# Rearranged start, output projection and shared weight buffers in a fused attention and MLP kernel

## The chip, the cores and the metric

The kernel runs on one core of a Trainium2 chip. The metric is the device time of one execution in microseconds (us). The core has a matrix engine (TensorE, PE in the profile, with its weight loads shown as PEld), a vector engine (VectorE, DVE), an activation engine (ScalarE, ACT), GpSimd (POOL) and a sync engine (SyncE, SP). In this kernel SP's queue issues every DMA.

## The reference

The input x has 2048 rows of 1024 values in bfloat16. The reference applies a layernorm, a dilated local attention with 32 heads of 32 values, and a residual addition, and then a second layernorm, a bilinear gated MLP with 3584 hidden values, and a second residual addition. Each position attends to eight positions: itself and those 2, 4, ... 14 rows earlier.

```python
h  = x + attention(layernorm(x), wqkv, wo)
h2 = h + mlp(layernorm(h), w_gate, w_up, w_down)

# attention: W, dil = 8, 2
idx    = pos[:, None] - arange(8)[None, :] * 2      # masked where negative
logits = einsum("bhsd,bhswd->bhsw", q, k[idx]) * 32 ** -0.5
o      = einsum("bhsw,bhswd->bhsd", softmax(logits), v[idx])
return o @ wo
# mlp
return ((x @ w_gate) * (x @ w_up)) @ w_down
```

## The kernel before

The 2048 rows are cut into 16 tiles of 128 rows. A tile holds rows of one parity: a tile is (sc, r), with sc the half of the sequence and r one of eight interleaved row numbers. Four tiles with the same half and the same parity make a block, so there are four blocks b of four tiles j. A tap at distance two rows is then the next tile of the same block.

The work has four kinds of steps.

- `A_ln(i)` loads tile i (xt, L205), normalises it on DVE and ACT (`layernorm_tile`, L93 to L105), transposes it on PE through PSUM (L209) and copies it to lnT on ACT (L211). `A_mm(i)` multiplies lnT with the six 512-column chunks of wqkv (48 matmuls, L223), copies each chunk to a staging tile on ACT (L226, L230) and stores the staging tile to a scratch tensor in DRAM (L232).
- `ATT(b)` does the attention of one block in four units of eight heads (`attention_unit`, L107 to L149). Each unit loads q_u, k_u and v_u from the scratch tensor (L112 to L114). DVE multiplies q with k and sums (L119 to L125), takes the softmax with one exponential on ACT (L132), multiplies with v and sums (L143 to L149). A unit reads v_u only after the softmax. The result is o_t, one tile for each j.
- `Ca(b, j)` transposes o_t on PE (L171), copies it to oT on ACT (L173), loads the tile of x again (L175), multiplies with wo (16 matmuls, L180), adds x on DVE (L182) and does the second layernorm. `Cb(b, j)` transposes the normalised tile (L190) and copies it into a quarter of ln2T_g on ACT (L191).
- `D_block(b, inserts)` is the MLP of one block. For each of seven groups of 512 hidden columns it loads wg_t and wu_t (1 MB each, L276 and L278), and computes four pairs of gate and up products (L282, L286), which need the whole ln2T_g. ACT copies the gate product (L289) and DVE multiplies it with the up product into hh (L291). Then two passes of seven groups read wd_t (L297) and accumulate four tiles at a time in PSUM (L301), and DVE adds the result to h_t (L305). After each down group, `inserts` may place steps of the next block's `Ca` and `Cb` (L307).

The program order is: `A_ln(0)`, the six loads of wqkv, then `A_ln(i + 1)` and `A_mm(i)` with `ATT` after every fourth tile; the tiles 13 to 15 are interleaved with `Ca` and `Cb` of block 0; then the four `D_block`s.

The framework plans the order of each engine's queue itself. It goes by priorities, which follow the program order except that `prio` (L55) puts all attention work behind everything else, by the expected times of instructions, and by free buffers: a tile of a pool with n buffers waits until the tile n allocations earlier is released. At run time each queue is worked off in its planned order. All PSUM tiles share eight buffers of one bank each (`psum`, tag "ps"). The wqkv chunks stand in a pool of their own for the time of the QKV stage (L195, L198); the MLP's pools (L262 to L265) are made after that stage's pools are closed, and lie in the same memory.

Of the kernel before, what the change touches and what calls it, by code (L numbers as in the profile page):

```python
# [8 lines left out]
BF = mybir.dt.bfloat16  # L9
# [5 lines left out]
S, D, H, DH, F, W = 2048, 1024, 32, 32, 3584, 8  # L15
P = 128
# [24 lines left out]
def kernel(  # L41
# [23 lines left out]
    small = ctx.enter_context(tc.tile_pool(name="small", bufs=4))  # L65
    psum = ctx.enter_context(tc.tile_pool(name="psum", bufs=8, space=bass.MemoryType.PSUM))
    au = ctx.enter_context(tc.tile_pool(name="au", bufs=2))
    wk = ctx.enter_context(tc.tile_pool(name="wk", bufs=2))
    sm = ctx.enter_context(tc.tile_pool(name="sm", bufs=1))
    op = ctx.enter_context(tc.tile_pool(name="op", bufs=2 * NJ))  # L70
    cp = ctx.enter_context(tc.tile_pool(name="cp", bufs=2))
    hp = ctx.enter_context(tc.tile_pool(name="hp", bufs=2 * NJ))
    lgp = ctx.enter_context(tc.tile_pool(name="lgp", bufs=2))

    nc.scalar.preload_act_table_set("natural_log_exp_and_others")
    ident = consts.tile([P, P], BF, name="ident")
# [30 lines left out]
    def attention_unit(sc, c, hq, o_tiles):  # L107
        row0 = PAD + sc * SCL + c
        q_u = au.tile([P, NJ, UW], BF, name="q_u")
        k_u = au.tile([P, NSLOT, UW], BF, name="k_u")  # L110
        v_u = au.tile([P, NSLOT, UW], BF, name="v_u")
        nc.sync.dma_start(q_u[:], dram_ap(scr, row0, hq * UW, [[R * NCOL, P], [2 * NCOL, NJ], [1, UW]]))  # L112
        nc.sync.dma_start(k_u[:], dram_ap(scr, row0 - 2 * (W - 1), D + hq * UW, [[R * NCOL, P], [2 * NCOL, NSLOT], [1, UW]]))
        nc.sync.dma_start(v_u[:], dram_ap(scr, row0 - 2 * (W - 1), 2 * D + hq * UW, [[R * NCOL, P], [2 * NCOL, NSLOT], [1, UW]]))  # L114
        L = sm.tile([P, NJ, W, NHU], F32, name="L")
        for j in range(NJ):
            prod = wk.tile([P, W, UW], BF, name="prod")
            qb = q_u[:, j:j + 1, :].to_broadcast((P, W, UW))
            nc.vector.tensor_tensor(prod[:], qb, k_u[:, j:j + W, :], ALU.mult)  # L119
            pv = prod[:].rearrange("p u (h d) -> p (u h) d", d=DH)  # L120
            t1 = wk.tile([P, W * NHU, 16], BF, name="t1")
            nc.vector.tensor_tensor(t1[:], pv[:, :, 0:16], pv[:, :, 16:32], ALU.add)  # L122
            t2 = wk.tile([P, W * NHU, 8], BF, name="t2")
            nc.vector.tensor_tensor(t2[:], t1[:, :, 0:8], t1[:, :, 8:16], ALU.add)  # L124
            nc.vector.tensor_reduce(L[:, j, :, :].rearrange("p u h -> p (u h)"), t2[:], AX.X, ALU.add)  # L125
        if sc == 0:
            nc.vector.tensor_tensor(L[:], L[:], mask_t[:].rearrange("p j (u o) -> p j u o", o=1).to_broadcast((P, NJ, W, NHU)), ALU.add)
        mx = sm.tile([P, NJ, NHU], F32, name="mx")
        nc.vector.tensor_reduce(mx[:], L[:].rearrange("p j u h -> p j h u"), AX.X, ALU.max)
        nc.vector.tensor_tensor(L[:], L[:], mx[:].rearrange("p j (o h) -> p j o h", o=1).to_broadcast((P, NJ, W, NHU)), ALU.subtract)  # L130
        E = sm.tile([P, NJ, W, NHU], F32, name="E")
        nc.scalar.activation(E[:], L[:], ACTF.Exp, scale=SCALE)  # L132
        den = sm.tile([P, NJ, NHU], F32, name="den")
        nc.vector.tensor_reduce(den[:], E[:].rearrange("p j u h -> p j h u"), AX.X, ALU.add)
        rden = sm.tile([P, NJ, NHU], F32, name="rden")
        nc.vector.reciprocal(rden[:], den[:])
        A = sm.tile([P, NJ, W, NHU], BF, name="A")
        nc.vector.tensor_tensor(A[:], E[:], rden[:].rearrange("p j (o h) -> p j o h", o=1).to_broadcast((P, NJ, W, NHU)), ALU.mult)
        for j in range(NJ):
            tmp = wk.tile([P, W, DH, NHU], BF, name="prod")  # L140
            vv = v_u[:, j:j + W, :].rearrange("p u (d h) -> p u d h", h=NHU)
            ab = A[:, j, :, :].rearrange("p u (o h) -> p u o h", o=1).to_broadcast((P, W, DH, NHU))
            nc.vector.tensor_tensor(tmp[:], vv, ab, ALU.mult)  # L143
# [5 lines left out]
            nc.vector.tensor_tensor(o_tiles[j][:, hq * UW:(hq + 1) * UW], s2[:, 0, :], s2[:, 1, :], ALU.add)  # L149
# [10 lines left out]

    cst = {}

    def Ca(b, j):
        sc, c = b // 2, b % 2
        r = 2 * j + c
        if j == 0:
            cst[b] = {"ln2T": lgp.tile([P, KT, 512], BF, name="ln2T_g"), "h": [None] * NJ, "ln2": [None] * NJ}
# [5 lines left out]
        nc.scalar.activation(oT[:], tp[:], ACTF.Copy)  # L173
# [18 lines left out]

    combs = [(b // 2, 2 * j + (b % 2), b) for b in range(NB) for j in range(NJ)]

    with tc.tile_pool(name="wq", bufs=1) as wqp, tc.tile_pool(name="pa", bufs=2) as pa, \  # L195
            tc.tile_pool(name="pax", bufs=3) as pax:
        wq_v = A_wqkv.rearrange("(kt k) n -> k kt n", k=P)
        wq = [wqp.tile([P, KT, 512], BF, name=f"wq{c}") for c in range(6)]  # L198
        lnTs = {}
        stages = {}  # L200

        def A_ln(i):
            sc, r, b = combs[i]
            xt = pax.tile([P, D], BF, name="xt")
            nc.sync.dma_start(xt[:], x_v[sc, :, r, :])  # L205
            ln = layernorm_tile(pa, xt, "ln1")
            tp = psum.tile([P, KT, P], BF, name="tp", tag="ps")
            for kt in range(KT):
                nc.tensor.transpose(tp[:, kt, :], ln[:, kt * P:(kt + 1) * P], ident[:])  # L209
            lnT = pa.tile([P, KT, P], BF, name="lnT")  # L210
            nc.scalar.activation(lnT[:], tp[:], ACTF.Copy)  # L211
            lnTs[i] = lnT

        def A_mm(i, chunks=range(6)):
            sc, r, b = combs[i]
            lnT = lnTs[i]
            if i not in stages:
                stages[i] = pa.tile([P, NCOL], BF, name="stage")
            stage = stages[i]
            for c in chunks:  # L220
                ps = psum.tile([P, 512], F32, name="ps", tag="ps")
# [9 lines left out]
            if chunks[-1] == 5:  # L231
                nc.sync.dma_start(scr_v[sc, :, r, :], stage[:])  # L232

        A_ln(0)
        for c in range(6):
            nc.sync.dma_start(wq[c][:], wq_v[:, :, c * 512:(c + 1) * 512])  # L236
        nc.sync.dma_start(scr[0:PAD, :].rearrange("a b -> (a b)").rearrange("(p f) -> p f", p=P), zt[:])
        for i in range(12):
            A_ln(i + 1)
            A_mm(i)  # L240
            if i == 1:
                for kt in range(KT):
                    hq_, kth = kt // 2, kt % 2
                    src = bass.AP(tensor=A_wo.tensor, offset=A_wo.offset + (hq_ * 256 + kth * 16) * D,
                                  ap=[[D, 16], [32 * D, NHU], [1, D]])
                    nc.sync.dma_start(wo_sb[:, kt, :], src)
            if i % NJ == NJ - 1:
                ATT(i // NJ)
        A_ln(13); A_mm(12)
        A_ln(14); A_mm(13)  # L250
        Ca(0, 0)
        A_ln(15); A_mm(14)
        Cb(0, 0); Ca(0, 1)
        A_mm(15, range(0, 2))
        Cb(0, 1); Ca(0, 2)
        A_mm(15, range(2, 4))
        Cb(0, 2); Ca(0, 3)
        A_mm(15, range(4, 6))
        Cb(0, 3)
        ATT(3)  # L260

    wgp = ctx.enter_context(tc.tile_pool(name="wgp", bufs=2))  # L262
    wdp = ctx.enter_context(tc.tile_pool(name="wdp", bufs=3))
    hhp = ctx.enter_context(tc.tile_pool(name="hhp", bufs=FT + 2))
    gp = ctx.enter_context(tc.tile_pool(name="gp", bufs=2))  # L265
    wg_v = B_w_gate.rearrange("(kt k) n -> k kt n", k=P)
    wu_v = B_w_up.rearrange("(kt k) n -> k kt n", k=P)
# [2 lines left out]
    def D_block(b, inserts):  # L270
# [1 line left out]
        h_ts, ln2T_g = cst[b]["h"], cst[b]["ln2T"]  # L272
        hh_tiles = []
        for fq in range(FT // 4):
            wg_t = wgp.tile([P, KT, 512], BF, name="wg_t")
            nc.sync.dma_start(wg_t[:], wg_v[:, :, fq * 512:(fq + 1) * 512])  # L276
# [35 lines left out]
    for b in range(NB):  # L312
        ins = {}
        if b + 1 < NB:
            nb = b + 1
            ins = {
                0: [lambda nb=nb: Ca(nb, 0)],
                2: [lambda nb=nb: Cb(nb, 0), lambda nb=nb: Ca(nb, 1)],
                4: [lambda nb=nb: Cb(nb, 1), lambda nb=nb: Ca(nb, 2)],
                6: [lambda nb=nb: Cb(nb, 2), lambda nb=nb: Ca(nb, 3)],  # L320
                8: [lambda nb=nb: Cb(nb, 3)],
            }
        D_block(b, ins)

# [29 lines left out]
```

## Time and profile before

| | before |
|---|---|
| time, median of 5 runs | 904.17 us (902.1 to 904.75) |
| time of the profiled execution | 904.75 us |
| span of the profiled execution | 903.0 us |
| mean granted TensorE clock | 0.986 |
| PE busy | 832.7 us (92%) |
| PE weight loads busy | 386.9 us (43%) |
| DVE busy | 534.3 us (59%) |
| ACT busy | 186.8 us (21%) |
| moved by DMA | 149.67 MB, mean 166 GB/s |

Busy time counts the time in which an engine has an instruction under way. PE's instructions overlap in a pipeline, and their recorded durations (about 380 ns for a 128x512 matmul) are longer than the distance between them, so PE's pace is better read from the starts of instructions. A line of the profile such as L223 is the line of the kernel that issued the instruction. "idle before <-X" tells how long an engine had nothing to do ahead of an instruction and what ended that time.

### The profile page before, as it was taken

To read this page: it belongs to the slowest core of one execution; us is meant where nothing else is said; L and a number is where in the kernel's file an instruction comes from. 1 tells how busy PE (TensorE), PEld (TensorE's weight loads), DVE (VectorE), ACT (ScalarE), POOL (GpSimd) and SP (SyncE) were. 2 spreads that over 40 slices of the span, in tenths; PEclk is the share of its full clock that TensorE was granted. 3 is DMA by queue.
4 is the path that set the end of the run, shared out by engine and by line. 5 is a ranking of instruction groups with operands and counts; after the bars stand their busy time and mean duration, and the time that the engine had idled before them with its cause. 6 is when DMAs were issued, how large, how long until landed. Compare 5 with 4: busy or idle time off the path is not lost.

```text
span 903.0 us, 10107 instructions
## 1 busy us (share of the span) xinstructions
PE 832.7 (92%) x4018; PEld 386.9 (43%) x4096; DVE 534.3 (59%) x907; ACT 186.8 (21%) x337; POOL 0.9 (0%) x7
## 2 busy tenths in 40 slices
PE   0899999976699999799999999999999999999997
PEld 0344444432344444344444444444444444444443
DVE  1424999999999999999999964021212322121111
ACT  1344434322211111210111112011111211111100
POOL 0000000000000000000000000000000000000000
PEclk9999999997899999999999999999999999999999
DMA  9737544432597676557675353454454334553053
GB/s 315 202 105 211 182 150 155 146 123 78 168 335 228 202 244 193 160 145 241 185 246 166 117 175 117 145 170 138 143 185 153 105 109 139 172 165 115 24 163 117
DMA packets 158624, 149.67 MB, mean 166 GB/s; under 512 B 3824, under 2 KB 149360, under 8 KB 158576
## 3 DMA queue, kind: packets, MB, share of 16 engines
q1 hardware_dynamic: 158576, 149.01, 52.8%
q8 instruction: 32, 0.52, 0.2%
q14 instruction: 16, 0.13, 0.0%
HBM read 132.12 MB, written 16.88 MB: 165 GB/s over the span
## 4 chain that ended last, share of the span: by engine, by line
PE 62%; DVE 27%; DMA 3%; issue 3%; ACT 2%; SPq 2%; DVEq 0%
PE pu L286 19%; PE pg L282 19%; PE acc L301 15%; PE ps L223 5%; DVE prod L143 4%; PE ps L180 4%; DVE prod L119 4%; DVE t L146 3%; DVE t L122 2%; DVE L L125 2%; DMA xt<-in_A_x_dram 1%; DVE t L124 1%; DVE t L148 1%; SPq L236 1%; DMA wu_t<-in_B_w_up_dram 1%
## 5 line engine op out<-in xcount | busy, mean ns | idle before, releaser
L282 PE MATMUL pg<-ln2T_g,wg_t 128*128 128x512 bf16 x876 | 211.7, 381 | 5.0 <-DMA wg_t<-in_B_w_gate_dram 3.9
L286 PE MATMUL pu<-ln2T_g,wu_t 128*128 128x512 bf16 x880 | 210.2, 379 | 2.0 <-DMA wu_t<-in_B_w_up_dram 1.2
L301 PE MATMUL acc<-wd_t,hh 128*128 128x512 bf16 x877 | 197.3, 380 | 1.6 <-DMA wd_t<-in_B_w_down_dram 0.4
L223 PE MATMUL ps<-wq,lnT 128*128 128x512 bf16 x750 | 169.7, 382 | 0.9
L291 DVE TENSOR_TENSOR hh<-pu,g_sb 128x512 bf16<-128x512 f32 x112 | 77.0, 688 | 152.5 <-PE pu L286 147.0
L289 ACT ACTIVATE g_sb<-pg 128x512 bf16<-128x512 f32 x112 | 66.4, 595 | 338.6 <-PE pg L282 265.1
L282 PEld LDWEIGHTS <-wg_t 128*128 128x128 bf16 x896 | 87.9, 98 | 110.5 <-issue 5.7
L286 PEld LDWEIGHTS <-wu_t 128*128 128x128 bf16 x896 | 87.6, 98 | 107.5 <-DMA wu_t<-in_B_w_up_dram 2.1
L301 PEld LDWEIGHTS <-hh 128*128 128x128 bf16 x896 | 87.4, 98 | 104.2 <-issue 2.0
L223 PEld LDWEIGHTS <-lnT 128*128 128x128 bf16 x768 | 75.1, 99 | 88.5 <-issue 2.5
L119 DVE TENSOR_TENSOR prod<-q_u,k_u 128x2048 bf16<-128x2048 bf16 x64 | 77.1, 1214 | 3.8 <-DMA k_u<-scr 3.8
L143 DVE TENSOR_TENSOR prod<-v_u,A 128x2048 bf16<-128x2048 bf16 x64 | 76.5, 1218 | 0.4
L180 PE MATMUL ps<-wo_sb,oT 128*128 128x512 bf16 x251 | 61.4, 400 | 15.6 <-ACT oT L173 15.0
L305 DVE TENSOR_TENSOR h_t<-acc,h_t 128x512 bf16<-128x512 f32 x32 | 19.9, 683 | 90.7 <-PE acc L301 90.7
L182 DVE TENSOR_TENSOR h_t<-ps,xt 128x512 bf16<-128x512 f32 x32 | 21.9, 685 | 44.5 <-PE ps L180 44.5
L180 PEld LDWEIGHTS <-oT 128*128 128x128 bf16 x256 | 24.9, 102 | 49.7 <-ACT oT L173 19.9
L226 ACT ACTIVATE stage<-ps 128x512 bf16<-128x512 f32 x64 | 36.5, 601 | 41.9 <-PE ps L223 40.6
L125 DVE TENSOR_REDUCE L<-t 128x64 f32<-128x512 bf16 x64 | 43.2, 679 | 0.5
L122 DVE TENSOR_TENSOR t<-prod 128x1024 bf16<-128x1024 bf16 x64 | 43.1, 680 | 0.0
L146 DVE TENSOR_TENSOR t<-prod 128x1024 bf16<-128x1024 bf16 x64 | 42.7, 683 | 0.0
L100 ACT ACTIVATE ln_lnv<-ln_mv,eps_t 128x1 f32<-128x1 f32 x32 | 9.4, 294 | 137.7 <-DVE ln_mv L98 137.7
L95 DVE BATCH_NORM_STATS2 ln_stats<-xt 128x6 f32<-128x512 bf16 x16 | 11.0, 687 | 44.0 <-DMA xt<-in_A_x_dram 44.0
(38 smaller groups left out, 308.1 us busy)
## 6 DMA issues: line engine op xcount, KB each, us to landing
wg_t<-in_B_w_gate_dram SPq DMA_DIRECT2D x28, 1024.0 KB, 5.4
wu_t<-in_B_w_up_dram SPq DMA_DIRECT2D x28, 1024.0 KB, 7.5
wd_t<-in_B_w_down_dram SPq DMA_DIRECT2D x56, 512.0 KB, 3.7
scr<-stage SPq DMA_DIRECT2D x16, 768.0 KB, 3.9
k_u<-scr SPq DMA_DIRECT2D x16, 704.0 KB, 5.5
v_u<-scr SPq DMA_DIRECT2D x16, 704.0 KB, 4.6
xt<-in_A_x_dram SPq DMA_DIRECT2D x32, 256.0 KB, 3.8
wq<-in_A_wqkv_dram SPq DMA_DIRECT2D x6, 1024.0 KB, 11.5
```

Source lines behind the costliest of these rows:

```text
L119: nc.vector.tensor_tensor(prod[:], qb, k_u[:, j:j + W, :], ALU.mult)
L122: nc.vector.tensor_tensor(t1[:], pv[:, :, 0:16], pv[:, :, 16:32], ALU.add)
L125: nc.vector.tensor_reduce(L[:, j, :, :].rearrange("p u h -> p (u h)"), t2[:], AX.X, ALU.add)
L143: nc.vector.tensor_tensor(tmp[:], vv, ab, ALU.mult)
L146: nc.vector.tensor_tensor(s1[:], tf[:, 0:4, :], tf[:, 4:8, :], ALU.add)
L180: nc.tensor.matmul(ps[:], oT[:, kt, :], wo_sb[:, kt, ch * 512:(ch + 1) * 512], start=(kt == 0), stop=(kt == KT - 1))
L223: nc.tensor.matmul(ps[:], lnT[:, kt, :], wq[c][:, kt, :], start=(kt == 0), stop=(kt == KT - 1))
L282: nc.tensor.matmul(pg[:], wg_t[:, kt, fi * P:(fi + 1) * P], ln2T_g[:, kt, :], start=(kt == 0), stop=(kt == KT - 1))
L286: nc.tensor.matmul(pu[:], wu_t[:, kt, fi * P:(fi + 1) * P], ln2T_g[:, kt, :], start=(kt == 0), stop=(kt == KT - 1))
L289: nc.scalar.activation(g_sb[:], pg[:], ACTF.Copy)
L291: nc.vector.tensor_tensor(hh[:], pu[:], g_sb[:], ALU.mult)
L301: nc.tensor.matmul(accs[jj][:], hh_tiles[ft][:, jj * P:(jj + 1) * P], wd_t[:, fi, :], start=(ft == 0), stop=(ft == FT - 1))
```

## The change

The change has these parts.

- The start runs three tiles (`NS = 3`) of `A_ln` ahead of the weight loads, and then takes the six chunks of wqkv one by one for all three tiles. `A_ln(3)` is placed after chunk 4. The staging tiles get three buffers in place of two, lnT four in place of two.
- The loads of wo move from after tile 1 to after tile 4.
- wqkv's six chunks and the gate and up weights now share one pool of six buffers of 8 KB per partition (`wbig`, tag "w8k"). Before, wqkv had six and gate and up had two each.
- `Ca` is split: `Ca1` transposes o_t, copies oT and loads x; `Ca2` does the product with wo, the addition and the layernorm. Other work is placed between the two, both at the end of the QKV stage and among the down groups of the MLP.
- v_u has one buffer in place of two, ln2T_g one in place of two, and hh 28 in place of 30.

```diff
...
+    auv = ctx.enter_context(tc.tile_pool(name="auv", bufs=1))
+    wbig = ctx.enter_context(tc.tile_pool(name="wbig", bufs=6))
...
-    lgp = ctx.enter_context(tc.tile_pool(name="lgp", bufs=2))
+    lgp = ctx.enter_context(tc.tile_pool(name="lgp", bufs=1))
...
-        v_u = au.tile([P, NSLOT, UW], BF, name="v_u")
+        v_u = auv.tile([P, NSLOT, UW], BF, name="v_u")
...
-    def Ca(b, j):
+    def Ca1(b, j):
...
         nc.sync.dma_start(xt2[:], x_v[sc, :, r, :])
+        cst[b]["oT"][j] = oT
+        cst[b]["xt2"][j] = xt2
+
+    def Ca2(b, j):
+        oT, xt2 = cst[b]["oT"][j], cst[b]["xt2"][j]
         h_t = hp.tile([P, D], BF, name="h_t")
...
-        wq = [wqp.tile([P, KT, 512], BF, name=f"wq{c}") for c in range(6)]
+        wq = [wbig.tile([P, KT, 512], BF, name=f"wq{c}", tag="w8k") for c in range(6)]
...
-            lnT = pa.tile([P, KT, P], BF, name="lnT")
+            lnT = pa4.tile([P, KT, P], BF, name="lnT")
...
-                stages[i] = pa.tile([P, NCOL], BF, name="stage")
+                stages[i] = pa3.tile([P, NCOL], BF, name="stage")
...
-        A_ln(0)
+        NS = 3
+        for i in range(NS):
+            A_ln(i)
         for c in range(6):
             nc.sync.dma_start(wq[c][:], wq_v[:, :, c * 512:(c + 1) * 512])
...
-        for i in range(12):
+        for c in range(6):
+            for i in range(NS):
+                A_mm(i, range(c, c + 1))
+            if c == 4:
+                A_ln(NS)
+        for i in range(NS, 12):
             A_ln(i + 1)
             A_mm(i)
-            if i == 1:
-                for kt in range(KT):
...
+            if i == 4:
+                load_wo()
...
         A_ln(14); A_mm(13)
-        Ca(0, 0)
-        A_ln(15); A_mm(14)
-        Cb(0, 0); Ca(0, 1)
+        Ca1(0, 0)
+        A_ln(15); A_mm(14, range(0, 3))
+        Ca2(0, 0); Ca1(0, 1)
+        A_mm(14, range(3, 6))
+        Ca2(0, 1); Cb(0, 0); Ca1(0, 2)
         A_mm(15, range(0, 2))
-        Cb(0, 1); Ca(0, 2)
+        Ca2(0, 2); Cb(0, 1); Ca1(0, 3)
         A_mm(15, range(2, 4))
-        Cb(0, 2); Ca(0, 3)
+        Ca2(0, 3); Cb(0, 2)
         A_mm(15, range(4, 6))
         Cb(0, 3)
         ATT(3)
 
-    wgp = ctx.enter_context(tc.tile_pool(name="wgp", bufs=2))
     wdp = ctx.enter_context(tc.tile_pool(name="wdp", bufs=3))
-    hhp = ctx.enter_context(tc.tile_pool(name="hhp", bufs=FT + 2))
+    hhp = ctx.enter_context(tc.tile_pool(name="hhp", bufs=FT))
...
-            wg_t = wgp.tile([P, KT, 512], BF, name="wg_t")
+            wg_t = wbig.tile([P, KT, 512], BF, name="wg_t", tag="w8k")
...
-            wu_t = wgp.tile([P, KT, 512], BF, name="wu_t")
+            wu_t = wbig.tile([P, KT, 512], BF, name="wu_t", tag="w8k")
...
-                0: [lambda nb=nb: Ca(nb, 0)],
-                2: [lambda nb=nb: Cb(nb, 0), lambda nb=nb: Ca(nb, 1)],
-                4: [lambda nb=nb: Cb(nb, 1), lambda nb=nb: Ca(nb, 2)],
-                6: [lambda nb=nb: Cb(nb, 2), lambda nb=nb: Ca(nb, 3)],
-                8: [lambda nb=nb: Cb(nb, 3)],
+                0: [lambda nb=nb: Ca1(nb, 0)],
+                1: [lambda nb=nb: Ca2(nb, 0), lambda nb=nb: Ca1(nb, 1)],
+                2: [lambda nb=nb: Ca2(nb, 1)],
+                3: [lambda nb=nb: Cb(nb, 0), lambda nb=nb: Ca1(nb, 2)],
+                4: [lambda nb=nb: Cb(nb, 1), lambda nb=nb: Ca2(nb, 2)],
+                7: [lambda nb=nb: Cb(nb, 2), lambda nb=nb: Ca1(nb, 3)],
+                8: [lambda nb=nb: Ca2(nb, 3)],
+                10: [lambda nb=nb: Cb(nb, 3)],
```

More of the change, by code (lines that the diff above doesn't have):

```diff
@@ L166, in Ca @@
         if j == 0:
-            cst[b] = {"ln2T": lgp.tile([P, KT, 512], BF, name="ln2T_g"), "h": [None] * NJ, "ln2": [None] * NJ}
+            cst[b] = {"ln2T": lgp.tile([P, KT, 512], BF, name="ln2T_g"), "h": [None] * NJ, "ln2": [None] * NJ,
+                      "oT": [None] * NJ, "xt2": [None] * NJ}
         o_t = o_all[b][j]
@@ L193 @@
     combs = [(b // 2, 2 * j + (b % 2), b) for b in range(NB) for j in range(NJ)]
-    with tc.tile_pool(name="wq", bufs=1) as wqp, tc.tile_pool(name="pa", bufs=2) as pa, \
-            tc.tile_pool(name="pax", bufs=3) as pax:
+    with tc.tile_pool(name="pa", bufs=2) as pa, tc.tile_pool(name="pa3", bufs=3) as pa3, \
+            tc.tile_pool(name="pa4", bufs=4) as pa4:
+        pax = pa3
         wq_v = A_wqkv.rearrange("(kt k) n -> k kt n", k=P)
-        wq = [wqp.tile([P, KT, 512], BF, name=f"wq{c}") for c in range(6)]
+        wq = [wbig.tile([P, KT, 512], BF, name=f"wq{c}", tag="w8k") for c in range(6)]
         lnTs = {}
@@ L230, in A_mm, with load_wo @@
                     nc.scalar.activation(dst, src, ACTF.Copy)
-            if chunks[-1] == 5:
+            if list(chunks)[-1] == 5:
                 nc.sync.dma_start(scr_v[sc, :, r, :], stage[:])
-        A_ln(0)
+        def load_wo():
+            for kt in range(KT):
+                hq_, kth = kt // 2, kt % 2
+                src = bass.AP(tensor=A_wo.tensor, offset=A_wo.offset + (hq_ * 256 + kth * 16) * D,
+                              ap=[[D, 16], [32 * D, NHU], [1, D]])
+                nc.sync.dma_start(wo_sb[:, kt, :], src)
+        NS = 3
+        for i in range(NS):
+            A_ln(i)
         for c in range(6):
```

4 lines of the change are left out of this document (removed).

## The prediction

> **What bounds the kernel now.** I read the page first, then TensorE's list of waits, then a table of busy time over eight stages that I cut at the places where TensorE (PE) changes its work, then the timelines around the stages that lose time.
>
> ```profile
> span 903.0 us, 10107 instructions
> PE tp L209 <- DVE ln_ln L104: 25.6, 2, 18.3
> PE ps L180 <- ACT oT L173: 15.0, 7, 5.3
> PE tp L190 <- DVE ln_ln L104: 12.8, 7, 5.1
> PE tp L171 <- DVE o_t L149: 1.5, 1, 1.5
> ```
>
> Each wait has its total, its count and its longest. The stages follow: bounds, length, then busy time (and instructions) of PE, weight load, DVE, ACT and POOL, then PE clock, DMA share and GB/s.
>
> ```profile
> 0.00:26.61 26.61, 1.03 (x8) 0.77 (x9) 5.52 (x14) 3.30 (x6) 0.89 (x7) 1.00 1.00 307
> 26.61:40.19 13.58, 13.53 (x64) 6.51 (x66) 6.14 (x14) 5.55 (x14) 0.00 (x0) 1.00 0.71 197
> 40.19:180.22 140.03, 139.34 (x710) 66.40 (x721) 103.18 (x180) 59.91 (x115) 0.00 (x0) 1.00 0.49 159
> 180.22:246.52 66.30, 44.22 (x228) 20.44 (x232) 62.42 (x110) 18.80 (x33) 0.00 (x0) 0.87 0.38 115
> 246.52:424.00 177.48, 167.03 (x791) 76.89 (x807) 173.90 (x295) 28.28 (x50) 0.00 (x0) 0.98 0.71 217
> 424.00:589.68 165.68, 162.95 (x790) 75.76 (x804) 120.23 (x203) 27.67 (x48) 0.00 (x0) 1.00 0.53 167
> 589.68:752.84 163.16, 160.43 (x778) 74.56 (x792) 36.72 (x59) 26.57 (x44) 0.00 (x0) 1.00 0.46 145
> 752.84:903.00 150.16, 144.14 (x659) 65.54 (x670) 26.21 (x40) 16.72 (x28) 0.00 (x0) 1.00 0.40 126
> ```
>
> PE is the bound in most stages, so what matters is how far each is from PE's own pace. A row of the chain and two transposes of neighbouring tiles give that pace:
>
> ```profile
> 261.79 1.73 PE pu L286 x8
> 50.55 0.61 PE L209 MATMUL tp<-ident,ln_ln 128*128 128x128 bf16 x8
> 61.35 0.61 PE L209 MATMUL tp<-ident,ln_ln 128*128 128x128 bf16 x8
> ```
>
> A 512-wide matmul takes 1.73/8 = 0.216 us. From 50.55 to 61.35 lie 48 of them (10.37) and 8 transposes, so eight transposes take 0.43. The program has 3712 such matmuls (768 QKV, 256 for wo, three times 896 in the MLP) and 384 transposes: 802 + 21 = 823 us. The other 80 us of the span are the target. By stage: the start loses 26; the stage 180 to 246 holds 160 matmuls and 72 transposes, 38.5 us of work in 66.3, a loss of 27.8; an MLP block with its insertions has 448 gate/up, 224 down and 64 wo matmuls and 64 transposes, 159.0 + 3.5 = 162.5, and the three stages from 246.52 to 752.84 total 506.3 against 487.5, a loss of 18.8, nearly all in the first. The stage 40 to 180 loses nothing.
>
> **The start: three tiles ahead of the weights.**
>
> ```profile
> 7.27 1.03 PE L209 MATMUL tp<-ident,ln_ln 128*128 128x128 bf16 x8 [7.27 <-DVE ln_ln L104]
> 8.35 1.02 ACT L211 ACTIVATE lnT<-tp 128x1024 bf16<-128x1024 bf16 x1 [1.71 <-PE tp L209]
> 26.61 1.04 PE L209 MATMUL tp<-ident,ln_ln 128*128 128x128 bf16 x8 [18.30 <-DVE ln_ln L104]
> 27.44 12.46 PE L223 MATMUL ps<-wq,lnT 128*128 128x512 bf16 x47
> 1.18 12.15 SPq L236 DMA_DIRECT2D wq<-in_A_wqkv_dram  x6
> 16.34 1.08 SPq L205 DMA_DIRECT2D xt<-in_A_x_dram  x2
> DMA to landing us min/median/max: 6.2/11.5/11.9
> 10.00:12.00 2.00, 0.00 (x0) 0.00 (x0) 0.00 (x0) 0.00 (x0) 0.00 (x0) 1.00 1.11 349
> ```
>
> PE has the first lnT at 9.4 and the first wq chunk has landed at 1.18 + 6.2 = 7.4 (the landing row is that of wq). Yet it sits until 26.61, because the transposes of the second tile stand ahead of the matmuls and their xt is issued at 16.34, behind six chunks of 1 MB. In the new order three xt go first: two more tiles of 256 KB at 349 GB/s put the first chunk at 8.9. Matmuls then start at 9.4 at the earliest; at the latest after the third tile's transposes, which need two more layernorms on DVE. All DVE work of the first stage is 5.52 us for two and more layernorms, so under 2.8 each: 7.3 + 5.6 + 0.6 = 13.5. I take the middle, 11.5. The chunk-major order uses 24 matmuls, 5.2 us, per chunk, and a chunk lands every 1.05 MB/349 = 3.0 us, so the weights stay ahead of PE. The move is 27.44 - 11.5 = 15.9, and the third transpose, now done by then, 0.4: **16.3 us** (14.3 to 18.5). The slow first matmuls (47 in 12.46) are paid in both.
>
> More lnT and stage buffers cost nothing. The eight wo loads go from tile 1 to tile 4, behind three more xt loads on SP; their first use, below, is at 183.65, and moving PE up by 16 leaves over 100 us. Attention of block 0 starts after tile 3 is stored, so it comes 16 us earlier along with PE.
>
> **The tail of QKV with block 0's output projection.**
>
> ```profile
> 182.25 0.29 PE L171 MATMUL tp<-ident,o_t 128*128 128x128 bf16 x2 [1.53 <-DVE o_t L149]
> 183.65 3.63 PE L180 MATMUL ps<-wo_sb,oT 128*128 128x512 bf16 x15 [1.12 <-ACT oT L173]
> 194.46 0.68 DVE L182 TENSOR_TENSOR h_t<-ps,xt 128x512 bf16<-128x512 f32 x1
> 199.78 0.62 PE L190 MATMUL tp<-ident,ln_ln 128*128 128x128 bf16 x8 [1.69 <-DVE ln_ln L104]
> 206.13 4.95 PE L180 MATMUL ps<-wo_sb,oT 128*128 128x512 bf16 x16 [5.28 <-ACT oT L173]
> 220.06 6.50 PE L180 MATMUL ps<-wo_sb,oT 128*128 128x512 bf16 x16 [1.58 <-ACT oT L173]
> 242.01 0.62 PE L190 MATMUL tp<-ident,ln_ln 128*128 128x128 bf16 x8 [1.75 <-DVE ln_ln L104]
> 246.52 3.49 PE L282 MATMUL pg<-ln2T_g,wg_t 128*128 128x512 bf16 x8 [3.88 <-DMA wg_t<-in_B_w_gate_dram]
> 251.25 1.90 PE L286 MATMUL pu<-ln2T_g,wu_t 128*128 128x512 bf16 x8 [1.24 <-DMA wu_t<-in_B_w_up_dram]
> 240.29 0.38 SPq L276 DMA_DIRECT2D wg_t<-in_B_w_gate_dram  x1
> ```
>
> Two things happen. Waits of under two us for oT follow each transpose of o_t, since nothing stands between them. And DVE runs late: the first half of wo's result is there by about 185.5 (8 matmuls after 183.65), the add starts at 194.46, 9 us later, with attention work queued ahead of it. That lag reaches PE once as layernorm and oT waits (1.69 and 5.28); PE then runs slowly, 16 matmuls in 4.95 and 6.50 instead of 3.46.
>
> The split puts 24 QKV matmuls (5.2 us) or a wo product (3.5) between transpose and product: the oT waits go. From a wo product to the transposes of its layernorm the new cover is 9.1 us for j=0 (chunks 3 to 5, the next product, transposes), 7.8 for j=1 and j=2, and 3.9 for j=3. Before, j=0 took 12.5 (187.3 to 199.8). So j=0 waits 3.4 in place of 1.7: the added wait has the transposes of tile 2 and two chunks queued behind it. I let the whole 9 us lag be absorbed by PE waits over the four tiles (the last has nearly no cover), keep the 1.5 for o_t and add 1.0 for ACT's copy before the first gate matmul: 11.5 of loss left, a gain of **16.3 us**. If every layernorm were in time, 3 would be left, a gain of 25; if the new waits are as long as the old, only 3.88 and the slow clock's half, 7 in all, are won.
>
> [...]
>
> wg and wu now share six buffers with wq, and the first two come free once tile 15 is through chunks 0 and 1, some 15 us of PE work before the first gate matmul. The first gate wait of 3.88 is in the sum above; the slow first group and the 1.24 behind it, 251.25 - 246.52 - 1.73 = 3.0, go too, in the next term. Gate, up and down weights are as many as before.
>
> **The MLP blocks.**
>
> ```profile
> 354.80 0.38 PE L180 MATMUL ps<-wo_sb,oT 128*128 128x512 bf16 x1
> 366.11 1.03 PE L190 MATMUL tp<-ident,ln_ln 128*128 128x128 bf16 x8 [5.10 <-DVE ln_ln L104]
> ```
>
> In block 0 the first layernorm takes 11 us from the product's end to its transposes (355.2 to 366.1), over a cover of two down groups (32 matmuls, 6.9). The new one is 10.8: two groups, a product and a transpose. If the lag of about 7 us is carried on, j=1 with a cover of 7.8 waits 3.3 and j=3 another 1; before, layernorm waits here were near 6 and oT, restarts and slow clock made 5 more. I take 6 us won here, 3.0 at the block's start, and 3 in blocks 1 and 2 together, where oT waits are what is left: **12 us**, between 5 and 17. Block 3 has no insertions and gains nothing.
>
> One ln2T buffer: it is rewritten in the down pass, after the last gate/up matmul of its block, so no wait. 28 hh buffers: the first is read for the last time early in the second down pass. hh now lies where the QKV staging tiles lay, so the first hh may wait for the last store; eight PSUM banks hold four pairs, 13.8 us of PE, over it.
>
> **One v_u buffer.**
>
> ```profile
> 82.88 2.36 DVE L119 TENSOR_TENSOR prod<-q_u,k_u 128x2048 bf16<-128x2048 bf16 x2 [3.76 <-DMA k_u<-scr]
> 186.86 2.35 DVE L119 TENSOR_TENSOR prod<-q_u,k_u 128x2048 bf16<-128x2048 bf16 x2
> 204.31 2.36 DVE L143 TENSOR_TENSOR prod<-v_u,A 128x2048 bf16<-128x2048 bf16 x2
> DMA to landing us min/median/max: 4.5/4.6/9.7
> ```
>
> The next unit's v_u is issued only when this unit is done, and first read after its scores and softmax: 186.86 to 204.31, 17 us. Landing (the row is that of v_u) takes 4.6, at most 9.7. I cost it at nothing; the cover is 17 - 9.7 = 7 us of delay on SP's queue. SP is in order, and xt, stores and weights stand behind the waiting load, as they do now behind the same load one unit later.
>
> Sum: 16.3 + 16.3 + 12 = 44.6. The profiled execution took 904.75 us (span 903.0), so 860.1; the median of the five is 904.17, 0.6 lower, so **859.5 us**.
>
> **The rivals.**
> (a) DVE's order decides: the waits in both insertion stages move instead of going. Then the start (16.3), the gate-weight waits (3.9 + 3.0) and 3 of slow clock remain: 26, or 878 us. For it: the 9 us between product and add. Against it: the longer covers.
> (b) Nearly all idle goes: 823 of work, 9.4 to 11.5 before it, 2 for the slow first matmuls, 6 behind the last matmul (as in the last stage, 150.2 against 145 for 672 matmuls), 3 of rest: 844.
> (c) The start doesn't move, because the planned order still puts a later tile's transposes ahead of the matmuls: 859.5 + 16 = 876.
> (d) Slower: v_u starves DVE. Late by x in each unit, it delays block 0's attention by 3x, and PE with it at o_t (182.25 shows PE already waiting there); block 1's four units can add 4x. The gain of 44.6 is gone at x = 6.4 (7x) to 15 (3x), so from 13 us on SP beyond landing in 17. At x = 8 it is 859.5 + 56 = 915. Against it: only one wait of PE for o_t today. [...]
>
> **How the numbers follow.** Forecast 0.60 (own range 850 to 868), (a) 0.18, (b) 0.10, (c) 0.08, (d) 0.04. The range 843 to 879 leaves out (d) and the far edges of (a) and (b). 0.2% is 1.8 us, about what a measurement can tell: faster 0.95, same 0.02, slower 0.03.
>
> **What would show it.** First QKV matmul at 9 to 13 us and no gap until 50; no wait of 18 us at L209; the stage from the end of tile 13 to the first gate matmul near 50 us instead of 66; that matmul waiting for ACT, not DMA; oT waits under 3 us in total; block 0 near 168. DVE waiting for v_u, or PE for o_t by more than some us, would make me wrong towards (d); long L190 waits towards (a).

## The result, and the profile after

The changed kernel takes 871.2 us (median of 9 runs, 870.3 to 872.4), against 902.9 for the kernel before (median of 16 runs): a ratio of 0.9649, 95% interval 0.9636 to 0.9662. That is 31.7 us faster; 44.6 had been forecast. The profiled execution has a span of 870.9 us, 32.1 shorter than before's, so the two traces can be compared as they are. First its span and PE's list of waits (total, count, longest). L218 is now the transpose of the first layernorm, L198 that of the second, L174 that of o_t, L188 the wo product, L302 and L306 gate and up, L321 the down product.

```profile
span 870.9 us, 10118 instructions
PE tp L198 <- DVE ln_ln L106: 10.5, 5, 4.1
PE tp L218 <- DVE ln_ln L106: 8.1, 3, 6.9
PE ps L188 <- ACT oT L176: 4.3, 3, 3.4
PE tp L174 <- DVE o_t L151: 1.9, 1, 1.9
PE ps L188 <- DVE h_t L190: 1.9, 1, 1.9
PE acc L321 <- DVE hh L311: 1.7, 1, 1.7
PE pg L302 <- ACT ln2T_g L199: 1.1, 1, 1.1
```

The 18.3 us wait at the start is gone, the oT waits fell from 15.0 to 4.3, and the waits for gate and up weights are gone. New are a wait for a sum on DVE (h_t), one for hh and one for the last copy to ln2T_g. Next come the stages of the changed kernel, cut at PE's own changes of work: the start, QKV up to the first transposes of o_t, the tail of QKV up to the first gate matmul, and the MLP blocks 0 to 3. The columns are as before: length, then PE, weight load, DVE, ACT, POOL, granted PE clock, DMA share and GB/s.

```profile
0.00:10.98 10.98, 2.89 (x24) 2.37 (x25) 6.00 (x15) 4.24 (x9) 0.89 (x7) 1.00 0.80 254
10.98:163.96 152.98, 152.24 (x757) 71.81 (x769) 108.20 (x190) 63.97 (x126) 0.00 (x0) 1.00 0.61 193
163.96:218.14 54.18, 42.27 (x228) 20.48 (x232) 53.21 (x96) 18.79 (x34) 0.00 (x0) 0.90 0.62 197
218.14:387.37 169.23, 163.96 (x784) 75.79 (x800) 165.25 (x279) 28.34 (x50) 0.00 (x0) 0.99 0.70 212
387.37:558.22 170.85, 163.95 (x786) 75.93 (x801) 135.50 (x230) 27.86 (x49) 0.00 (x0) 0.99 0.57 177
558.22:720.64 162.42, 161.58 (x785) 75.59 (x800) 38.44 (x61) 26.67 (x44) 0.00 (x0) 1.00 0.46 146
720.64:870.90 150.26, 144.52 (x660) 65.68 (x671) 26.38 (x40) 16.72 (x28) 0.00 (x0) 1.00 0.35 112
```

Block 2 takes 162.42, which is PE's own pace to a tenth. Block 1 got longer: 170.85, where it took 164.89 before, from its first gate matmul to the next block's. This is the row of the kernel before for the same stage, and PE's one wait of more than half a us in it:

```profile
422.90:587.79 164.89, 162.16 (x786) 75.38 (x800) 119.44 (x201) 27.67 (x48) 0.00 (x0) 1.00 0.54 168
559.93 3.40 PE L180 MATMUL ps<-wo_sb,oT 128*128 128x512 bf16 x15 [1.81 <-ACT oT L173]
```

DVE was busy 119.4 us in that stage; it is 135.5 now, and 38.4 in block 2. The table sets the stages of all kernels side by side. "Tail" runs from the first o_t transposes to the first gate matmul, a block from its first gate matmul to the next block's; PE's own pace is 38.5 and 162.5.

| kernel | time, us | ratio to before, 95% interval | tail | block 0 | block 1 | block 2 |
|---|---|---|---|---|---|---|
| before | 902.9 | | 66.3 | 176.4 | 164.9 | 164.9 |
| changed | 871.2 | 0.9649 (0.9636 to 0.9662) | 54.2 | 169.2 | 170.9 | 162.4 |
| e1, new start alone | 884.4 | 0.9795 (0.9775 to 0.9814) | 64.2 | 176.0 | 164.9 | 164.9 |
| e2, old start | 887.6 | 0.9830 (0.9811 to 0.9849) | 53.6 | 170.4 | 169.1 | 162.4 |
| e3, old insertions | 881.3 | 0.9759 (0.9739 to 0.9779) | 54.9 | 172.4 | 174.1 | 164.9 |
| e4, old tail | 873.2 | 0.9668 (0.9645 to 0.9691) | 62.3 | 168.7 | 164.3 | 162.4 |
| e5, own weight pools | 872.4 | 0.9666 (0.9647 to 0.9685) | 61.5 | 170.5 | 164.4 | 162.4 |
| e6, two v_u buffers | 871.9 | 0.9658 (0.9639 to 0.9676) | 53.8 | 170.6 | 169.2 | 162.4 |
| e7, oT early | 871.9 | 0.9656 (0.9636 to 0.9675) | 53.5 | 170.6 | 170.0 | 162.4 |
| e8, lighter attention | 862.8 | 0.9556 (0.9539 to 0.9572) | 54.0 | 168.6 | 162.4 | 162.4 |
| e9, later steps in block 1 | 865.9 | 0.9601 (0.9584 to 0.9619) | 54.7 | 170.0 | 164.3 | 162.4 |
| e10, one attention | 845.6 | 0.9378 (0.9363 to 0.9393) | 44.2 | 162.4 | 162.4 | 162.4 |
| e11, later steps in blocks 0, 1 | 866.4 | 0.9604 (0.9588 to 0.9620) | 54.0 | 169.7 | 165.3 | 162.4 |
| e12, and four wd buffers | 866.5 | 0.9589 (0.9566 to 0.9612) | 54.0 | 169.4 | 164.0 | 162.4 |

The start first, on PE's timeline (start, length, then the idle time ahead):

```profile
10.16 1.04 PE L218 MATMUL tp<-ident,ln_ln 128*128 128x128 bf16 x8 [0.96 <-DVE ln_ln L106]
10.98 28.64 PE L232 MATMUL ps<-wq,lnT 128*128 128x512 bf16 x118
39.46 0.61 PE L218 MATMUL tp<-ident,ln_ln 128*128 128x128 bf16 x8
```

The third tile's transposes at 10.16 set the first matmul, at 10.98, and 120 matmuls follow without a gap: 28.5 us where 25.9 is PE's pace, so 2.6 go to the slow beginning. Now the tail: PE, then ACT, then DVE.

```profile
175.99 5.34 PE L232 MATMUL ps<-wq,lnT 128*128 128x512 bf16 x23
184.75 6.33 PE L188 MATMUL ps<-wo_sb,oT 128*128 128x512 bf16 x16 [3.41 <-ACT oT L176]
207.79 0.62 PE L198 MATMUL tp<-ident,ln_ln 128*128 128x128 bf16 x8 [1.11 <-DVE ln_ln L106]
216.00 1.03 PE L198 MATMUL tp<-ident,ln_ln 128*128 128x128 bf16 x8 [4.13 <-DVE ln_ln L106]
218.14 3.27 PE L302 MATMUL pg<-ln2T_g,wg_t 128*128 128x512 bf16 x8 [1.11 <-ACT ln2T_g L199]
183.36 0.42 ACT L134 ACTIVATE E<-L 128x256 f32<-128x256 f32 x1 [10.47 <-DVE L L132]
183.69 1.00 ACT L176 ACTIVATE oT<-tp 128x1024 bf16<-128x1024 bf16 x1
183.19 0.68 DVE L190 TENSOR_TENSOR h_t<-ps,xt 128x512 bf16<-128x512 f32 x1
```

The transposes of o_t's second tile end by 175.99, and 5.2 us of matmuls stand behind them, as intended. But on ACT's queue the exponential of the next attention unit stands ahead of the oT copy, and waits 10.5 us for DVE. PE waits 3.41 and then does 16 matmuls in 6.33, at a granted clock of 0.56 (184.75 to 191.00); the same 16 take 3.62 at 172.09, at full pace. On DVE the first sum of the wo product runs at 183.19; the product's first half was done at about 174 (8 matmuls after 172.09). That is the 9 us lag again. Last, block 1's down pass:

```profile
486.55 2.97 PE L321 MATMUL acc<-wd_t,hh 128*128 128x512 bf16 x13 [1.67 <-DVE hh L311]
504.37 1.89 PE L188 MATMUL ps<-wo_sb,oT 128*128 128x512 bf16 x7 [1.88 <-DVE h_t L190]
515.95 0.62 PE L198 MATMUL tp<-ident,ln_ln 128*128 128x128 bf16 x8 [1.89 <-DVE ln_ln L106]
517.19 5.31 PE L188 MATMUL ps<-wo_sb,oT 128*128 128x512 bf16 x16 [0.62 <-ACT oT L176]
503.63 0.68 DVE L190 TENSOR_TENSOR h_t<-ps,xt 128x512 bf16<-128x512 f32 x1
514.36 0.27 DVE L151 TENSOR_TENSOR o_t<-t 128x256 bf16<-128x256 bf16 x1
```

The four waits (6.1 together) and the slow 16 matmuls behind the last of them (1.7) make up 7.8 of the 8.4 us that block 1 takes beyond PE's own pace. The last o_t of block 3 is written at 514.4. The down pass begins at 484, so its first 30 us share DVE with attention. Before, the last o_t was written at 526.9 and the pass began at 519.6, so only 7 us were shared. PE had come forward by 36 us, attention by 12.5.

### The profile page after: what moved, and what is told of

It reads as the page before. It is cut to its first block, busy times and chain, and to the rows that moved or that the text cites. A ratio compares the mean times of both kernels' runs of the same rounds, so it can differ in the third digit from the quotient of the medians.

```text
span 870.9 us, 10118 instructions
## 1 busy us (share of the span) xinstructions
PE 831.4 (95%) x4016; PEld 387.6 (45%) x4096; DVE 533.0 (61%) x907; ACT 186.6 (21%) x337; POOL 0.9 (0%) x7
## 4 chain that ended last, share of the span: by engine, by line
PE 59%; DVE 34%; issue 4%; DMA 2%; ACT 1%; DVEq 0%; SPq 0%; ACTq 0%
PE pg L302 17%; PE pu L306 17%; PE acc L321 16%; PE ps L232 5%; DVE prod L145 5%; DVE prod L121 5%; DVE t L148 3%; DVE t L124 3%; DVE L L127 3%; PE ps L188 3%; DVE hh L311 2%; DVE t L150 2%; DVE t L126 2%; DVE h_t L190 1%; DVE ln_stats L97 1%
## 5 line engine op out<-in xcount | busy, mean ns | idle before, releaser
L302 PE MATMUL pg<-ln2T_g,wg_t 128*128 128x512 bf16 x876 | 210.7, 381 | 2.0 <-ACT ln2T_g L199 1.1
L306 PE MATMUL pu<-ln2T_g,wu_t 128*128 128x512 bf16 x880 | 210.2, 379 | 1.1
L321 PE MATMUL acc<-wd_t,hh 128*128 128x512 bf16 x877 | 197.1, 379 | 2.7 <-DVE hh L311 1.7
L302 PEld LDWEIGHTS <-wg_t 128*128 128x128 bf16 x896 | 88.0, 98 | 107.7 <-issue 2.9
L306 PEld LDWEIGHTS <-wu_t 128*128 128x128 bf16 x896 | 87.7, 98 | 105.8 <-issue 0.2
L321 PEld LDWEIGHTS <-hh 128*128 128x128 bf16 x896 | 87.1, 98 | 104.0 <-issue 2.0
L188 PE MATMUL ps<-wo_sb,oT 128*128 128x512 bf16 x250 | 62.3, 400 | 6.6 <-ACT oT L176 4.3
L188 PEld LDWEIGHTS <-oT 128*128 128x128 bf16 x256 | 25.8, 102 | 40.0 <-issue 8.5
```

The source lines that it names most:

```text
L188: nc.tensor.matmul(ps[:], oT[:, kt, :], wo_sb[:, kt, ch * 512:(ch + 1) * 512], start=(kt == 0), stop=(kt == KT - 1))
L302: nc.tensor.matmul(pg[:], wg_t[:, kt, fi * P:(fi + 1) * P], ln2T_g[:, kt, :], start=(kt == 0), stop=(kt == KT - 1))
L306: nc.tensor.matmul(pu[:], wu_t[:, kt, fi * P:(fi + 1) * P], ln2T_g[:, kt, :], start=(kt == 0), stop=(kt == KT - 1))
L321: nc.tensor.matmul(accs[jj][:], hh_tiles[ft][:, jj * P:(jj + 1) * P], wd_t[:, fi, :], start=(ft == 0), stop=(ft == FT - 1))
```

## The experiments

### The parts one by one

e1 is the kernel before with the new start, the later loads of wo and the buffers that the start needs.

```diff
...
-        A_ln(0)
...
+        NS = 3
+        for i in range(NS):
+            A_ln(i)
...
-        for i in range(12):
+        for c in range(6):
+            for i in range(NS):
+                A_mm(i, range(c, c + 1))
...
```

> The kernel before with the new start alone (three tiles ahead of the weights, chunk by chunk, with the lnT and staging buffers that it needs). If the start is a gain of PE and of attention alike, since attention begins after tile 3, the time falls by 16 us, to 887. If attention on DVE doesn't move along, PE waits for o_t at the end of QKV and the gain is under 10 us, over 893.

884.4 us, 19 less than before, where 16 had been expected: by the traces 17.3 are won up to the first o_t transposes (162.9, before 180.2) and 2.1 in the tail. PE waits 2.3 us for o_t. Attention moves along: its last o_t is written at 507.7 (526.9 before).

e2 takes the same lines back out of the changed kernel.

```diff
-        for i in range(NS):
-            A_ln(i)
+        A_ln(0)
...
```

> The changed kernel with the old start. If the start is worth the same with and without the other parts: 871 + 16 = 887. If its gain is partly given back in block 1's down pass, where attention is still running in the changed kernel, the old start costs less than 13 us, under 884.

887.6 us: 16.4 more than the changed kernel. The start is worth about the same alone (19) and with the other parts (16). Its gain isn't given back, because attention comes forward with PE: without the new start the last o_t (530.2) and the down pass of block 1 (500.0) both come 16 us later.

e3 puts the steps in the down passes back to their old places.

```diff
...
-                1: [lambda nb=nb: Ca2(nb, 0), lambda nb=nb: Ca1(nb, 1)],
-                2: [lambda nb=nb: Ca2(nb, 1)],
...
+                0: [lambda nb=nb: Ca1(nb, 0), lambda nb=nb: Ca2(nb, 0)],
+                2: [lambda nb=nb: Cb(nb, 0), lambda nb=nb: Ca1(nb, 1), lambda nb=nb: Ca2(nb, 1)],
...
```

> The changed kernel with block steps inserted at the old places of the down passes and Ca undivided there. If the loss of 8 us in block 1 comes from attention that is still on DVE, the old places lose as much there as block 0 lost before, about 12, and block 0 loses 5 more, block 2 2.5 more: 871 + 5 + 4 + 2.5 = 882. If it comes from the new places themselves, block 1 wins 6 back: 873 or less.

881.3 us; blocks 0, 1 and 2 take 3.2, 3.2 and 2.5 more. The new places win against the old in every block, in block 1 too; its loss is larger with the old places (11.6 beyond PE's pace) than with the new (8.4).

e4 puts the end of QKV back to its old order.

```diff
-        Ca1(0, 0)
-        A_ln(15); A_mm(14, range(0, 3))
-        Ca2(0, 0); Ca1(0, 1)
-        A_mm(14, range(3, 6))
-        Ca2(0, 1); Cb(0, 0); Ca1(0, 2)
+        Ca1(0, 0); Ca2(0, 0)
+        A_ln(15); A_mm(14)
+        Cb(0, 0); Ca1(0, 1); Ca2(0, 1)
...
```

> The changed kernel with the old order at the end of QKV. If the longer covers of the new order are what took the waits away, the stage from the first o_t transposes to the first gate matmul gets about 8 us longer, 66 less the 4 for gate weights, and the time is 879. If the new order only put one wait (oT behind the exponential on ACT's queue) in place of others, the time stays within 2 us of 871.

873.2 us: 2 more, which the intervals don't tell from nothing. Yet the tail did get 8.1 longer, as the first expectation said. The next rows are e4's tail and its block 1:

```profile
163.42:225.67 62.25, 43.14 (x233) 20.12 (x232) 59.72 (x107) 19.00 (x34) 0.00 (x0) 0.92 0.58 180
394.41:558.72 164.31, 162.75 (x801) 75.52 (x800) 129.36 (x217) 27.67 (x48) 0.00 (x0) 1.00 0.57 177
```

Block 1 ends at 558.72, and in the changed kernel at 558.22. What the new order wins in the tail is given back two blocks later.

e5 gives wqkv, gate and up pools of their own, as before.

```diff
...
-            wg_t = wbig.tile([P, KT, 512], BF, name="wg_t", tag="w8k")
+            wg_t = wgp.tile([P, KT, 512], BF, name="wg_t")
...
```

> The changed kernel with wqkv in a pool of its own and two buffers each for gate and up, as before. If the shared buffers are what lets the first gate weights land early, the first gate matmul waits for DMA again, some 4 us, and restarts slowly, some 2: 877. If the layernorm of the last tile is what holds the first gate matmul anyway, 871 to 873.

872.4 us. PE's first gate matmul, then the tail and block 1:

```profile
225.06 3.57 PE L302 MATMUL pg<-ln2T_g,wg_t 128*128 128x512 bf16 x8 [7.59 <-DMA wg_t<-in_B_w_gate_dram]
163.56:225.06 61.50, 41.32 (x229) 20.01 (x233) 60.25 (x109) 20.00 (x36) 0.00 (x0) 0.90 0.45 143
395.58:560.00 164.42, 161.90 (x786) 75.53 (x800) 128.99 (x217) 27.56 (x48) 0.00 (x0) 1.00 0.57 177
```

The weights come 7.6 us late, so the shared buffers do what they seem to, and the tail is 7.3 longer. Again block 1 is 6.4 shorter and ends within 2 us of the same moment. The result fits the second expectation in its number but not in its reason. e4 and e5 have the same thing in common: the down pass of block 1 begins 7 and 8 us later than in the changed kernel (491.1 and 492.3), and the last o_t is written 5 and 4 us earlier (509.3 and 510.6), so that 18 us of the pass lie beside attention in place of 30.

e6 has two v_u buffers.

```diff
-    auv = ctx.enter_context(tc.tile_pool(name="auv", bufs=1))
+    auv = ctx.enter_context(tc.tile_pool(name="auv", bufs=2))
```

> The changed kernel with two v_u buffers. If one buffer costs nothing, as DVE never waited for v_u in the trace, 871 within 2 us. If the single buffer shifts loads on SP's queue enough to hold other work, 868 or less.

871.9 us, no difference. In the changed kernel's trace nothing waits for v_u.

### Where DVE's lateness sits

e7 moves the second tile's o_t transposes ahead of tile 14's matmuls.

```diff
-        A_ln(15); A_mm(14, range(0, 3))
-        Ca2(0, 0); Ca1(0, 1)
+        A_ln(15); Ca1(0, 1); A_mm(14, range(0, 3))
+        Ca2(0, 0)
```

> The changed kernel with the o_t transposes of tile 1 moved ahead of chunks 0 to 2 of tile 14, so that both oT copies stand on ACT's queue ahead of the exponential of the next attention unit. If that exponential, which waits 10 us for DVE, is the cause of the 3.4 us oT wait and the slow matmuls behind it, these 6 us go: 865. If DVE's lateness is kept whatever stands on ACT's queue, the layernorm of tile 0, which is ready at 189.5, holds PE instead and 1 to 2 us are won: 870.

871.9 us. Two of PE's waits and the tail:

```profile
PE tp L198 <- DVE ln_ln L106: 12.9, 4, 6.0
PE ps L188 <- ACT oT L176: 1.2, 3, 0.6
163.38:216.91 53.53, 41.57 (x230) 20.87 (x232) 52.78 (x95) 18.66 (x33) 0.00 (x0) 0.93 0.59 188
```

The oT wait of 3.4 is gone and the layernorm waits have grown. The exponential on ACT's queue decided at which step PE waited; it did not decide how long the tail took.

e8 leaves out the multiplication of v by the attention weights.

```diff
...
-                nc.vector.tensor_tensor(tmp[:], vv, ab, ALU.mult)
-                tf = tmp[:].rearrange("p u d h -> p u (d h)")
+                tf = v_u[:, j:j + W, :]
```

> The changed kernel without the multiplication of v by the attention weights (64 instructions of 1.2 us on DVE are left out, the sums over v stay). If DVE's late order behind attention makes the losses, the tail's 15.7 falls to about 6, block 0's 6.7 to 2, block 1's 8.3 to 1: 871 - 21 = 850. If the losses are the latencies of the steps themselves (ACT copies, layernorm chain), at most 6 us go: 865 or more.

862.8 us, between the two. Tail, block 0 and block 1:

```profile
163.78:217.74 53.96, 41.07 (x229) 20.88 (x233) 53.92 (x106) 19.37 (x36) 0.00 (x0) 0.90 0.67 212
217.74:386.34 168.60, 164.67 (x784) 76.06 (x800) 165.27 (x317) 29.46 (x52) 0.00 (x0) 0.98 0.77 231
386.34:548.77 162.43, 161.59 (x786) 75.58 (x801) 53.37 (x91) 26.98 (x45) 0.00 (x0) 1.00 0.48 154
```

Attention is over before block 1's down pass, and block 1's loss of 8.4 is gone to the tenth. The tail and block 0 did not change, because there DVE is as full as before (53.9 of 54.0 us, 165 of 168.6) with the attention that follows. How much attention there is decides where it ends; that some is always queued decides the tail and block 0.

e10 leaves out the attention of blocks 1 to 3, with its loads and exponentials, and halves the o_t buffers; their projection reads block 0's.

```diff
...
+        if b > 0:
+            o_all[b] = o_all[0]
+            return
```

> The changed kernel with the attention of blocks 1 to 3 left out: their output projection reads block 0's attention. DVE has nothing but layernorms, sums and hh after block 0's attention. If attention ahead of the layernorm work on DVE's queue makes the losses of the tail (15.7) and of block 0 (6.7), the tail takes 40 to 44 and block 0 163 to 164: about 871 - 11 - 6 - 8 = 846. If the tail's losses are its own latencies (o_t to oT, product to layernorm, the restart of the clock), the tail stays above 50 and the time above 853.

845.6 us, as the first expectation said. Tail and block 0, then PE at the beginning of the tail:

```profile
162.38:206.59 44.21, 40.32 (x229) 20.15 (x233) 21.78 (x39) 19.16 (x33) 0.00 (x0) 0.96 0.52 173
206.59:369.01 162.42, 161.58 (x784) 75.59 (x800) 36.32 (x57) 26.68 (x44) 0.00 (x0) 1.00 0.51 164
165.36 0.29 PE L177 MATMUL tp<-ident,o_t 128*128 128x128 bf16 x2 [2.48 <-DVE o_t L151]
165.93 7.03 PE L235 MATMUL ps<-wq,lnT 128*128 128x512 bf16 x23
```

Without attention beside them, the new orders leave no layernorm and no oT wait at all. In the tail 5.7 us remain: 2.5 for o_t, 1.7 of slow matmuls behind that wait, 1.2 for ACT's copy and small terms. So 10 of the tail's 15.7 and all of block 0's 6.7 come from attention. That it is the part on DVE is read from the waits: in the changed kernel PE waits for DMA in neither stage.

### Moving the steps instead

e9 leaves the places of block 0 and 2 and moves block 1's steps later.

```diff
...
+            4: [lambda: Ca1(nb, 0)],
+            5: [lambda: Ca2(nb, 0), lambda: Ca1(nb, 1)],
+            6: [lambda: Ca2(nb, 1)],
+            8: [lambda: Cb(nb, 0), lambda: Ca1(nb, 2)],
+            9: [lambda: Cb(nb, 1), lambda: Ca2(nb, 2), lambda: Ca1(nb, 3)],
+            10: [lambda: Ca2(nb, 3)],
+            11: [lambda: Cb(nb, 2)],
+            12: [lambda: Cb(nb, 3)],
...
```

> The changed kernel with the steps of block 2 placed later in block 1's down pass: first o_t transposes after group 4 in place of 0, the last layernorm transposes after group 12 in place of 10. Nothing else is moved. If block 1's loss of 8.4 us is the meeting of these steps with attention, which holds DVE until 514, some 6 us go: block 1 takes 164 to 165 and the time is 865. If DVE is late in block 1 as a whole (hh at the end of the gate/up part, sums of the first down pass), block 1 stays at 170 and the time at 871.

865.9 us, ratio 0.9601 (0.9584 to 0.9619), faster than both kernels. Block 1, and PE's first layernorm transposes in its down pass:

```profile
387.47:551.72 164.25, 161.74 (x786) 75.54 (x800) 136.41 (x230) 28.32 (x49) 0.00 (x0) 1.00 0.59 184
524.87 0.61 PE L198 MATMUL tp<-ident,ln_ln 128*128 128x128 bf16 x8
```

DVE has as much to do as in the changed kernel (136.4 against 135.5), but PE doesn't ask for a layernorm until 524.87, 16 us after the last o_t (508.9). Of the 8.4 us, 6.6 are gone; only the wait for hh stays (1.7).

e11 adds longer covers in block 0: more matmuls between a layernorm's start and its transposes.

```diff
...
+                4: [lambda: Cb(nb, 0), lambda: Ca1(nb, 2)],
+                5: [lambda: Ca2(nb, 2)],
+                8: [lambda: Cb(nb, 1), lambda: Ca1(nb, 3)],
+                9: [lambda: Ca2(nb, 3)],
+                10: [lambda: Cb(nb, 2)],
+                12: [lambda: Cb(nb, 3)],
...
```

> The kernel with late steps in block 1, and in block 0 longer covers for the layernorms: tile 0's transposes after group 4 in place of 3, tile 1's after group 8 in place of 4, tile 2's after 10 in place of 7, tile 3's after 12 in place of 10. If block 0's waits for layernorms (2.5, 0.9, 0.7 and what stands around them) are covers that are too short, block 0 goes from 170.0 to 166 and the time from 866 to 862. If DVE's late order passes any cover, or the PE time won here only meets attention later in block 1, 865 to 866.

866.4 us, no gain over e9. PE in block 0, and SP's queue:

```profile
352.59 12.21 PE L321 MATMUL acc<-wd_t,hh 128*128 128x512 bf16 x47 [2.18 <-DMA wd_t<-in_B_w_down_dram]
342.32 0.34 SPq L178 DMA_DIRECT2D xt<-in_A_x_dram  x1
344.25 0.37 SPq L116 DMA_DIRECT2D v_u<-scr  x1
344.70 2.85 SPq L317 DMA_DIRECT2D wd_t<-in_B_w_down_dram  x3
```

The layernorm waits of block 0 are gone, but now a down weight is late. Its buffer is free after the first pass's fourth group, at about 339, and its load is issued at 344.70: it stands behind the load of x for the next step, which waits for a sum on DVE until 342.32, and then behind v_u's. The last run, e12, is e11 with a fourth buffer for wd.

```diff
-    wdp = ctx.enter_context(tc.tile_pool(name="wdp", bufs=3))
+    wdp = ctx.enter_context(tc.tile_pool(name="wdp", bufs=4))
```

> The kernel with later steps in blocks 0 and 1, with four wd buffers in place of three. There block 0 had no layernorm wait left, but PE waited 2.2 us for a wd load, which stood on SP's queue behind the v_u load that waits for the end of an attention unit, and ran slowly for 1.7 behind it. If that queue is what took back the gain, a load issued one group earlier brings 3 to 4: block 0 at 166, the time at 862. If the next late thing on DVE holds PE instead, block 0 or block 1 gets longer by as much and the time stays at 866.

866.5 us. The wait for wd is gone, and PE waits for a PSUM bank that a late sum on DVE frees:

```profile
355.58 0.38 PE L321 MATMUL acc<-wd_t,hh 128*128 128x512 bf16 x1 [2.10 <-DVE h_t L190]
```

Block 0 takes 169.4. With different waits in it (layernorms in the changed kernel and in e9, a down weight in e11, a sum in e12) it keeps to between 169.2 and 170.0.

## Why the prediction was right, and which terms were wrong

The time of 871.2 lies outside the forecast's own range (850 to 868) and inside the whole (843 to 879), which the rivals had widened. The direction was right, and so was the start; the other terms won less than forecast, and one of them lost.

**The start** was to win 16.3, and PE comes to the first o_t transposes 16.3 us earlier (163.96 against 180.22). The mechanism was right; that it agrees to a tenth is partly luck. The first matmul was put in the middle of a bracket of 4 us and came half a us sooner (10.98, not 11.5), and the stretch up to the o_t transposes lost that half again: it took 153.0 where 152.4 was implied, the old 152.8 less the third transposes. In the trace PE waits for none of v_u, the ln2T buffer, the 28 hh buffers or the later wo loads; only v_u was tested alone (e6). Rival (d) did not occur.

**The tail** was to win 16.3 and won 12.1: 15.7 of loss stayed instead of 11.5. The mis-sized term is the lag, of which I let PE absorb 9 us. PE's waits for oT and the layernorms come to 8.7 (3.4, 1.1 and 4.1), and the slow stretch behind the first of them takes 2.7 more (6.33 in place of 3.62); the rest of the 4.2 is in small terms, such as 1.9 in place of 1.5 for o_t and slow transposes at the end. That the waits alone come so near to 9 is luck, for the first came at oT and not at the layernorm. The slow stretch is not what makes the tail long, as e12 shows. It has the same program in the tail and the same wait, but no slow stretch behind it; the second row is its whole tail:

```profile
185.19 3.63 PE L188 MATMUL ps<-wo_sb,oT 128*128 128x512 bf16 x16 [3.41 <-ACT oT L176]
164.14:218.17 54.03, 39.49 (x228) 19.30 (x232) 53.48 (x96) 19.06 (x34) 0.00 (x0) 0.99 0.62 197
```

Its granted clock is 0.99, the changed kernel's 0.90, and its tail takes 54.0 as well: PE's waits for oT and the layernorms sum to 11.0 there (3.4, 1.2, 0.6, 1.6 and 4.1). DVE's last layernorm in the tail ends its work at nearly the same time in both (its last step starts at 215.84 there, at 215.40 here). The time that PE doesn't lose to slow matmuls it waits for DVE, so the lag costs some 11 us either way. The forecast's sum has no term for a slow stretch behind a new wait. The changed kernel's trace shows one of 2.7, but the length of the tail did not hang on it.

**Block 0** was to win 9 (3 at its start and 6 later) and won 7.2. Its first gate group was slow again, behind the waits at the tail's end: 3.1 (218.14 to 221.25) after 4.7 before, so 1.6 of the 3 were won, and 5.6 of the 6. Its longest layernorm wait is at the second tile, where it was forecast: 2.5 in place of 3.3.

**Blocks 1 and 2** were to win 3 together, and lost 3.5: block 2 won 2.5, block 1 lost 6.0. This is the step that failed. I took block 1's waits from the old trace, where oT waits are what is left and the down pass meets a DVE that finishes attention 7 us into it, and moved only PE. PE came forward by 36 us up to there and attention by 12.5. e8 and e9 show the cause from two sides: attention ending earlier takes all of the 8.4 us beyond PE's pace away, steps asking later 6.6 of it. What the new order and the shared buffers win in the tail mostly went there: e4 and e5 lose 8.1 and 7.3 in the tail, and 2.0 and 1.2 in all.

Rival (a), that DVE's order decides and waits move instead of going, was right about the mechanism in the tail (e7, e12) and fits block 1, for which it had no price. Its 878 let all the waits stay in the tail and in block 0, where part of them did go. The four terms give 16.3 + 12.1 + 7.2 - 3.5 = 32.1, the difference of the spans.

Left open is why DVE runs 9 us behind the moment at which PE delivers. The order on its queue is planned ahead of the run, and the runs show only that attention stands before the sums; no run changed the planned order alone.

## What to carry to other kernels

When PE is moved forward past an engine that stays full, look up which work of that engine will now lie beside each later stage, and re-price the waits there with the moved clock, not with the old trace. A stage's gain counts only once the next meeting point with the full engine has been checked: here 8 us won in one stage were worth 2. If several edits remove different waits and the stage keeps its length, suspect the order of the full engine's work: here asking it later (e9) or giving it less (e8, e10) helped, and another buffer (e6, e12) did not. A slow stretch of PE may cost nothing where PE would wait for that engine anyway: with 2.7 us of it behind the oT wait the tail took 54.2 (changed kernel), without it 54.0 (e12).

## What the runs showed of the hardware that was not expected

A PE wait of 2.48 us in e10 was followed by 24 matmuls in 6.9 us in place of 5.2 (165.93), at a granted clock of 0.76, while a wait of 1.89 at the same place in the changed kernel was followed by 24 in 5.2 (166.91 to 172.09), at 1.00.

In these runs the length of the wait alone does not decide. The same wait of 3.41 us for oT in the tail was followed by 16 matmuls in 6.33 us in the changed kernel, in 5.31 in e6 and in 3.63 in e12, at granted clocks of 0.56, 0.67 and 1.00. A wait of 2.49 us in block 0 of the changed kernel (345.12) was followed by 16 in 3.63. Which waits do it is not settled.
